# Loading w1 first as four full rows a partition, and three smaller edits, in a fused decode attention and Mish MLP kernel

## The chip, the cores and the metric

The kernel runs on one core of a Trainium2 chip. The metric is the time of one execution on the device in microseconds. Times of operations, waits and transfers are from the hardware profile of one execution of the kernel before the change.

## The reference

For 8 sequences with one new token each, the block adds to its input an attention over a long cache and a two-layer MLP, both fed with the same layer norm. All tensors are float32. Cut to what matters:

```python
x                # [8, 1, 512]
k_cache, v_cache # [8, 8, 8192, 128]   268 MB each
wq, wo           # [512, 4096], [4096, 512]
w1, b1, w2       # [512, 1792], [1792], [1792, 512]

xn = layernorm(x)
q = (xn @ wq) in 32 heads of 128; four heads share one key/value head
p = softmax(q @ k_cache^T * 128**-0.5)
a = (p @ v_cache) @ wo
h = xn @ w1 + b1
m = (h * tanh(softplus(h))) @ w2
out = x + a + m
```

## The kernel before, in words

The host lays the arrays out, and the kernel streams them through on-chip memory once. One *unit* is one sequence and two of its eight key/value heads: 8.4 MB of keys and 8.4 MB of values, each brought in by one DMA over all 128 partitions, 64 KB a partition. There are 32 units.

On-chip, one tile `kv` holds 2.5 such loads a partition. Values go to its start (`V_AT`). Keys go alternately to two places (`K_AT`) that overlap by half: the upper half of the first is the lower half of the second. A key load therefore starts once half of the unit before it has been multiplied. A second tile, `ws`, holds one quarter of wq (2.1 MB).

The order of work is written by hand. A loop of 17 steps runs `odd(t)` and then `even(t)`, a unit each; its last step runs `last()` instead of `even`. In a unit, `scores` multiplies the two halves of the keys with the unit's weights `wk` (32 products, which appear as 64 instructions, since each float32 product is two); `softmax` works on the VectorE and ScalarE; `values` does the value products of the unit before; `turn` and the VectorE behind it bring the probabilities into the form that `values` needs. Loads are issued from the SP queue, in the program's order, and an issue waits until what it overwrites has been read. Because SP works through its list in order, a load that waits holds up the loads behind it.

The MLP is spread out around this:

- Ahead of the loop (the *prologue*) the layer norm of x is made and transposed to `xn4`, which holds x's rows p*4+i in partition p. `project` makes the first queries from the first quarter of wq. `x_rows` and `x_turn` make `x8`, a second transposed copy of x with zeros in it, in the form that w1's layout needs. Its constant is `hmask`.
- w1 comes in one DMA, queued behind the first unit's keys: every partition gets eight half rows (`W1R = 8`), into the place of the values, which is still free.
- `up` makes h from w1 in 32 products of 448 columns, in `even(0)`, between the first unit's softmax and its `turn`. The first load of values, which overwrites w1, is issued once `up` is done. h stays in the accumulator bank `H` until `mish` reads it in `odd(1)`.
- In `last()`, the four parts of wo and then w2 are loaded in six parts (14 rows a partition: 4, 4, 3, 2 and the last row in two halves), all of w2 into the upper half of the second key place. `down_long` multiplies the first four rows in products of 512 columns into `H`; then ScalarE copies `H` to `a_sb`, four products with `bsel` bring it to the accumulator `O`, and `down` adds rows 5 to 14 to `O` in products of 128 columns. VectorE adds x, and the result is stored.

```python
    for p, t in zip(parts[1:], w2_t[1:]):
        down(p[0], p[1], t, p[2], p[3])
    res = os
    nc.vector.tensor_add(res, O[:, :P], xres)
    nc.sync.dma_start(out, res)
```

Of the kernel before, what the change touches and what calls it, by code (L numbers as in the profile page):

```python
# [8 lines left out]
F32 = mybir.dt.float32  # L9
AF = mybir.ActivationFunctionType  # L10
ALU = mybir.AluOpType
AX = mybir.AxisListType

P = 128
B = 8
D = 512
# [8 lines left out]
G = 4  # L25
# [3 lines left out]
CC = D // P  # L29
FG = F // G  # L30
FT = 4
FP = FG // FT
Q = P // G
# [15 lines left out]
NJ = PL * HALF  # L49


W1R = 8
W2R = 7


# [3 lines left out]
W1_AT = 0  # L59
W2_AT = 2 * ROW  # L60
# [15 lines left out]
def kernel(  # L76
# [12 lines left out]
    nc = tc.nc  # L89
    PSUM = bass.MemoryType.PSUM  # L90

    const = ctx.enter_context(tc.tile_pool(name="const", bufs=1))
# [4 lines left out]
    kv = const.tile([P, PLACES], F32, name="kv")  # L97
    ws = const.tile([P, CC * BW], F32, name="ws")
# [4 lines left out]
    M = psum.tile([P, 512], F32, name="m")  # L103
    H = psum.tile([P, 512], F32, name="h")
# [12 lines left out]
    apart = const.tile([P, P], F32, name="apart")  # L117
    gsel = const.tile([G, G, B], F32, name="gsel")
    xn4 = const.tile([P, CC, B], F32, name="xn4")
    hmask = const.tile([P, 2], F32, name="hmask")  # L120
    qr = const.tile([P, DI, H2 * B], F32, name="qr")
    xres = const.tile([P, P], F32, name="xres")
    oT = const.tile([P, H2, B], F32, name="oT")
    oX = const.tile([P, NP, CC, 2, B], F32, name="oX")

    x8 = oX.rearrange("p m i h b -> p (m i h b)")[:, : W1R * 2 * B]
    x8 = x8.rearrange("p (i h b) -> p i h b", i=W1R, h=2)
    aT = const.tile([P, 2 * W2R, B], F32, name="aT")
    pt8 = const.tile([P, HALF, PL * TL, H2], F32, name="pt8")
    tr = const.tile([P, PL * TL, 32], F32, name="tr")  # L130

    wk = const.tile([P, DI, 2, NH * G, REP], F32, name="wk")
    xe = wk.rearrange("p i d k h -> p (i d k h)")[:B].rearrange("b (i s) -> b i s", i=W1R)

    def load_q(m):

        rows = wq.rearrange("j p f -> (j p f)").rearrange("(m p f) -> m p f", m=NP, p=P)
# [14 lines left out]
    for lo in range(0, FG, FG // 2):  # L152
        hi = lo + FG // 2
        nc.scalar.dma_start(b1_sb[:, lo:hi], b1.rearrange("(g f) -> g f", g=G)[:, lo:hi])
    nc.sync.dma_start(
        kv[:, K_AT[0] : K_AT[0] + ROW],
        kT[:NB].rearrange("j p f -> (j p f)").rearrange("(p f) -> p f", p=P),
    )
    w1_t = kv[:, W1_AT : W1_AT + 7168].rearrange("p (i f) -> p i f", i=W1R)


    make_identity(nc, ident)
# [7 lines left out]

    def more_constants():
        nc.vector.reduce_sum(mask, ident.rearrange("p (x d) -> p x d", x=NB), axis=AX.X)
        nc.vector.reduce_sum(
            hmask, ident.rearrange("p (c h q) -> p h c q", c=CC, h=2), axis=AX.XY
        )
        nc.vector.memset(O, 0.0)
        for g in range(4):

            src = ident.rearrange("p (c d u g h) -> p d u g c h", c=2, d=2, u=2, g=4)
            dst = perm[:, g].rearrange("p (d u g c h) -> p d u g c h", d=2, u=2, g=4, c=2)  # L180
            for d in range(2):
                nc.vector.tensor_copy(dst[:, d, :, g], src[:, d, :, g])
        nc.vector.reduce_sum(hsel, ident.rearrange("p (c h) -> p h c", h=H2), axis=AX.X)
        nc.vector.reduce_sum(
            isel, ident.rearrange("p (c t h) -> p t c h", t=TL, h=H2), axis=AX.XY
        )
        for d in range(2):
            nc.vector.reduce_sum(
                rsel[:, d * REP : (d + 1) * REP],
                ident.rearrange("p (c d k h) -> p d h c k", c=2, d=2, h=REP)[:, d],  # L190
                axis=AX.XY,
            )
        away = work.tile([P, H2], F32, name="away", bufs=1)
        nc.vector.tensor_scalar(away, rsel, -FAR, FAR, op0=ALU.mult, op1=ALU.add)
        for c in range(2):
            nc.vector.tensor_copy(
                apart.rearrange("p (c d k h) -> p c d k h", c=2, d=2, h=REP)[:, c],
                away.rearrange("p (d o h) -> p d o h", d=2, o=1).to_broadcast([P, 2, NH * G, REP]),
            )
        nc.vector.tensor_copy(  # L200
            gsel, ident[:G, :G].rearrange("p (g o) -> p g o", o=1).to_broadcast([G, G, B])
        )
# [31 lines left out]
            gmask.rearrange("p (o g) -> p o g", o=1).to_broadcast([P, NB, DG]),  # L234
        )

    def x_rows():

        for c in range(CC):
            nc.vector.tensor_copy(
                xe.rearrange("b i (c h q) -> b c i h q", c=CC, h=2)[:, c],
                xc[:, c * P : (c + 1) * P]
                .rearrange("b (o q i) -> b i o q", o=1, i=W1R)
                .to_broadcast([B, W1R, 2, P // CC // 2]),
            )

    def x_turn():
        for i in range(W1R):  # L250
            nc.tensor.transpose(M[:, 32 + i * B : 32 + (i + 1) * B], xe[:, i], ident[:B, :B])
        for g in range(G):
            nc.tensor.matmul(
                M[Q * g : Q * g + B, 256:384],
                ident[:B, :B],
                x_sb[:, g * P : (g + 1) * P],
                start=True,
                stop=True,
            )
        for h in range(2):  # L260
            nc.vector.tensor_scalar(
                x8[:, :, h],
                M[:, 32 : 32 + W1R * B].rearrange("p (i b) -> p i b", i=W1R),
                hmask[:, h : h + 1],
                None,
                op0=ALU.mult,
            )
        nc.vector.tensor_copy(xres, M[:, 256:384])

    selections_long()  # L270
    x_rows()
    more_constants()


# [194 lines left out]
    def up(w1_t, b1_sb):  # L469
        for g in range(G):  # L470
            nc.tensor.matmul(
                hp[Q * g : Q * g + B, :], gsel[:, g, :], b1_sb, start=True, stop=False
            )
        for i in range(W1R):
            for g in range(G):
                nc.tensor.matmul(
                    hp[Q * g : Q * g + B, :],
                    x8[:, i, g // 2],
                    w1_t[:, i, g % 2 * FG : (g % 2 + 1) * FG],
                    start=False,  # L480
                    stop=(i == W1R - 1),
                )
# [42 lines left out]
                stop=False,  # L525
            )

    def down_long(w):

        for j in range(G):  # L530
            nc.tensor.matmul(
                H[Q * j : Q * j + B, :],
                aT[:, j, :],
                w[:, j * D : (j + 1) * D],
                start=False,
                stop=True,
            )

    def down(lo, hi, w, g0, g1):
        n = (g1 - g0) * P  # L540
        for j in range(lo, hi):
            for g in range(g0, g1):
                at = (j - lo) * n + (g - g0) * P
                nc.tensor.matmul(
                    O[Q * g : Q * g + B, :P],
                    aT[:, j, :],
                    w[:, at : at + P],
                    start=False,
                    stop=(j == 2 * W2R - 1),
                )  # L550

# [10 lines left out]
    def load(name, at, m, b):  # L562
        nc.sync.dma_start(place(at), units[name][m, b])  # L563

    nc.sync.dma_start(w1_t, w1.rearrange("j p f -> (j p f)").rearrange("(p i f) -> p i f", p=P, i=W1R))
    nc.sync.dma_start(place(K_AT[1])[:, ROW // 2 :], units["k"][0, 1][:, ROW // 2 :])
    project(work.tile([P, 512], F32, name="e", bufs=1))
    load_q(1)
    x_turn()
    spread()  # L570
    key_weights(0, 2)

    def last():

        w_o = [kv[:, 4096 * m : 4096 * (m + 1)] for m in range(NP)]
        for m in range(NP):
            rows = wo[4 * m : 4 * (m + 1)].rearrange("u p f -> (u p f)")
            rows = rows.rearrange("(p f) -> p f", p=P)
            nc.sync.dma_start(w_o[m], rows)
        w2_rows = w2.rearrange("j p f -> (j p) f").rearrange("(q i) f -> q (i f)", i=W2R)  # L580
        w2_t = []
        parts = ((0, G, 0, G), (G, 8, 0, G), (8, 11, 0, G), (11, 13, 0, G), (13, 14, 0, 2), (13, 14, 2, G))
        for lo, hi, g0, g1 in parts:
            a, z = (lo * D, hi * D) if g1 - g0 == G else (lo * D + g0 * P, lo * D + g1 * P)
            t = kv[:, W2_AT + a : W2_AT + z]
            nc.sync.dma_start(t, w2_rows[:, a:z])  # L586
            w2_t.append(t)

        values(place(K_AT[0]))
        for m in range(NP):  # L590
            if m == 1:
                merge(1, B - 1)
                turn_o(NP - 1)
            outputs(m, w_o[m])
        down_long(w2_t[0])
        a_sb = work.tile([P, 512], F32, name="e", bufs=1)
        nc.scalar.copy(a_sb, H)
        for g in range(G):
            nc.tensor.matmul(
                O[Q * g : Q * g + B, :P],  # L600
                bsel[:, :B],
                a_sb[:, g * P : (g + 1) * P],
                start=True,
                stop=False,
            )
        for p, t in zip(parts[1:], w2_t[1:]):
            down(p[0], p[1], t, p[2], p[3])
        res = os
        nc.vector.tensor_add(res, O[:, :P], xres)  # L609
        nc.sync.dma_start(out, res)  # L610
# [24 lines left out]
    def even(t):  # L635
# [14 lines left out]
        with tc.If(t > 0):  # L650
            values(place(V_AT))
        key_weights((2 * t + 1) % B)
        with tc.If(t == 0):  # L653
            up(w1_t, b1_sb)
        load("v", V_AT, t // 4 % NP, 2 * t % B)
        with tc.If(t % 4 - t // B * 4 == 3):
            load_q((t // 4 + 2) % NP)
# [49 lines left out]
```

## Time and profile before

| | |
|---|---|
| three runs: median (lowest to highest) | 1310.69 us (1310.49 to 1312.02) |
| the profiled execution | 1309.59 us |
| its span in the profile | 1307.8 us |
| TensorE busy, matmul | 992.6 us, 76% |
| VectorE busy | 359.0 us, 27% |
| DMA bytes | 561.33 MB, mean 429 GB/s |

Busy times are sums over the span, and the engines work side by side. A time at the start of a row of the timeline is microseconds from the start of the span. "xN" counts instructions, and a bracket at the end of a row gives how long the engine had been idle and what ended that. A row of SPq is the issue of a load; "to landing" is the time from the issue to the last byte.

### The profile page before, as it was taken

The numbers are of one execution on the slowest core, as the hardware profiler recorded it, in microseconds if no ns is written. First come the engines' busy times: TensorE is split into PE (matmuls) and PEld (weight loads), VectorE is DVE, ScalarE is ACT, GpSimd is POOL, SyncE is SP. The second block draws the span as 40 slices with busy tenths as digits, with TensorE's granted clock in tenths as the row PEclk, the third lists the DMA queues.
The fourth block names the chain that finished last, engine by engine and source line by source line (L and its number), as shares of the span: only waits on it lengthen the run. The fifth ranks groups of instructions, "written<-read, shape, count | busy, mean of one in ns | idle before, by whom it ended". The sixth has DMA issues, their size and how long they took to land. (4 is left out here: it accounts for less than half of the span.)

```text
span 1307.8 us, 15745 instructions
## 1 busy us (share of the span) xinstructions
PE 992.6 (76%) x4948; PEld 359.8 (28%) x4948; DVE 359.0 (27%) x654; ACT 39.3 (3%) x89; POOL 2.3 (0%) x10
## 2 busy tenths in 40 slices
PE   4887788778678688786686878878686878868686
PEld 2232223222222223222232322223232232323222
DVE  3215233221223302233312323212233231323312
ACT  1000000000000000000000000000000000000000
POOL 0000000000000000000000000000000000000000
PEclk9988898898888988998998888889888898988888
DMA  9999999999999999999999999999999999999998
GB/s 404 436 414 426 438 425 443 423 441 427 439 429 437 429 437 433 429 439 429 437 429 439 429 437 425 441 427 439 427 439 427 439 429 437 431 435 433 433 422 336
DMA packets 11857, 561.33 MB, mean 429 GB/s; under 512 B 1328, under 2 KB 1720, under 8 KB 1984
## 3 DMA queue, kind: packets, MB, share of 16 engines
q1 hardware_dynamic: 11680, 560.03, 99.2%
q10 hardware_dynamic: 160, 1.06, 0.2%
q8 instruction: 13, 0.21, 0.1%
q14 instruction: 4, 0.03, 0.0%
HBM read 561.01 MB, written 0.07 MB: 429 GB/s over the span
## 5 line engine op out<-in xcount | busy, mean ns | idle before, releaser
L373 PE MATMUL s<-kv,wk 128*64 128x512 f32 x2048 | 538.0, 664 | 195.7 <-DMA kv<-in_kT 108.2
L373 PEld LDWEIGHTS s<-kv,wk 128*64 128x64 f32 x2048 | 180.5, 151 | 521.7 <-issue 459.8
L428 PE MATMUL o<-kv,pt 128*32 128x512 f32 x2048 | 257.6, 659 | 31.1 <-DMA kv<-in_v 26.2
L385 DVE TENSOR_REDUCE nm<-s 128x1 f32<-128x512 f32 x32 | 22.1, 692 | 529.0 <-PE s L373 350.7
L399 PE MATMUL x<-e,perm 128*128 128x512 f32 x256 | 117.6, 602 | 26.5 <-PEq L653 15.0
L428 PEld LDWEIGHTS o<-kv,pt 128*32 128x32 f32 x2048 | 80.5, 120 | 184.8 <-issue 178.6
L408 DVE STREAM_TRANSPOSE tr<-x 128x512 f32<-128x512 f32 x128 | 79.2, 676 | 26.0 <-PE x L399 18.6
L435 DVE TENSOR_SCALAR os<-o,isel 128x128 f32<-128x128 f32 x32 | 11.2, 351 | 230.9 <-PE o L428 205.8
L399 PEld LDWEIGHTS x<-e,perm 128*128 128x128 f32 x256 | 46.0, 190 | 97.2 <-issue 96.9
L356 DVE TENSOR_TENSOR wk<-qr,mask 128x1024 f32<-128x1024 f32 (+1 forms) x34 | 65.1, 1915 | 12.9 <-DVEq L625 6.8
L393 ACT ACTIVATE e<-s,nmx 128x512 f32<-128x512 f32 x32 | 22.0, 687 | 1016.6 <-DVE nmx L390 1016.6
L417 DVE TENSOR_TENSOR pt<-tr 64x512 f32<-64x512 f32 x64 | 43.9, 687 | 4.4
L386 PE MATMUL m<-ident,nm 128*128 128x128 f32 x64 | 18.4, 375 | 28.4 <-DVE nm L385 28.4
L413 DVE TENSOR_TENSOR tr<-tr 128x1024 f32<-128x1024 f32 x32 | 39.2, 1225 | 1.1
L437 DVE SCALAR_TENSOR_TENSOR os<-o,isel,os 128x128 f32<-128x128 f32 x96 | 33.7, 351 | 3.4
L386 PEld LDWEIGHTS m<-ident,nm 128*128 128x128 f32 x64 | 11.4, 222 | 62.3 <-DVE nm L385 62.3
L442 PE MATMUL m<-hsel,os 128*128 128x8 f32 x64 | 10.9, 242 | 9.8 <-DVE rt L406 9.7
L442 PEld LDWEIGHTS m<-hsel,os 128*128 128x128 f32 x64 | 10.8, 189 | 19.4 <-DVE rt L406 11.3
L394 DVE TENSOR_SCALAR lsel<-rsel,l 128x8 f32<-128x8 f32 x32 | 7.4, 231 | 29.7 <-ACT e L393 15.8
L388 DVE TENSOR_TENSOR far<-m,apart 128x128 f32<-128x128 f32 x32 | 9.3, 292 | 21.3 <-PE m L386 21.3
L326 DVE TENSOR_SCALAR qT<-m 128x64 f32<-128x64 f32 x3 | 0.7, 225 | 51.1 <-PE m L319 51.1
L337 PE MATMUL x<-tr,gwide 128*128 128x512 f32 x16 | 10.9, 768 | 4.3 <-ACT qr L344 2.9
(106 smaller groups left out, 153.1 us busy)
## 6 DMA issues: line engine op xcount, KB each, us to landing
kv<-in_kT SPq DMA_DIRECT2D x2, 4096.0 KB, 32.8
kv<-in_wo SPq DMA_DIRECT2D x4, 2048.0 KB, 19.7
ws<-in_wq SPq DMA_DIRECT2D x3, 2048.0 KB, 33.3
kv<-in_w SPq DMA_DIRECT2D x1, 3584.0 KB, 35.5
kv<-in_w SPq DMA_DIRECT2D x2, 1024.0 KB, 27.6
ws<-in_wq ACTq DMA_DIRECT2D x1, 1024.0 KB, 5.1
ws<-in_wq SPq DMA_DIRECT2D x1, 1024.0 KB, 7.2
kv<-in_w SPq DMA_DIRECT2D x1, 768.0 KB, 26.4
```

The source lines that it names most:

```text
L356: nc.vector.tensor_mul(w[:, i : i + n], q[:, i : i + n].to_broadcast([P, n, 2, NH * G, REP]), mask.rearrange("p (o d k r) -> p o d k r", o ...
L373: nc.tensor.matmul(S[64 * c : 64 * (c + 1), :], w[:, i].rearrange("p d k h -> p (d k h)"), kk[:, i, c, :], start=(part == 0 and n == 0), s ...
L385: nc.vector.tensor_reduce(nm, S, axis=AX.X, op=ALU.max, negate=True)
L386: nc.tensor.matmul(M[:, 0:P], nm.to_broadcast([P, P]), ident, start=True, stop=True)
L393: nc.scalar.activation(e, S, AF.Exp, bias=nmx, accum_out=l)
L399: nc.tensor.matmul(X[:, g], perm[:, g], e, start=True, stop=True)
L408: nc.vector.transpose(tr.rearrange("p (l t) c -> p t l c", t=TL)[:, tl], X.rearrange("p g (t q l) -> p t l g q", t=TL, q=PP)[:, tl],)
L413: nc.vector.tensor_add(t[:, :, 0], t[:, :, 0], t[:, :, 1])
L417: nc.vector.tensor_add(pt8[half, :, :, d * REP : (d + 1) * REP].rearrange("p c y h -> p y c h"), t[:, 0], t[:, 1],)
L428: nc.tensor.matmul(O[Q * q : Q * (q + 1), :], pt8[:, c, TL * l : TL * (l + 1), :].rearrange("p t h -> p (t h)"), vt[:, 512 * n : 512 * (n ...
L437: nc.vector.scalar_tensor_tensor(os, O[:, DH * i : DH * (i + 1)], isel[:, i : i + 1], os, op0=ALU.mult, op1=ALU.add)
L442: nc.tensor.matmul(M[:, 168 : 168 + H2], os, hsel, start=True, stop=True)
```

## The change: w1 first, and its products in the prologue

Four edits:

1. w1's load is issued ahead of the first keys instead of behind them, and in another form. A partition now gets four full rows (`W1R = 4`), which are the rows that `xn4` already pairs with it. Since w1 lies in memory by blocks of 128 rows and by halves of its columns, it is now four DMAs, each into 32 of the 128 partitions, two runs of 14,336 bytes a partition. Before it was one DMA into 128 partitions, 28,672 bytes each.
2. `up` moves from `even(0)` to the prologue, and has 16 products instead of 32. `x8`, `xe`, `hmask`, `x_rows` and the eight transposes of `x_turn` are gone.
3. In `last()`, rows 5 to 8 of w2 are multiplied by `down_long` (4 products of 512 columns) instead of `down` (16 of 128). The copy of `H` comes behind them, and `down` does rows 9 to 11 ahead of the `bsel` products instead of behind.
4. w2's last row goes to `ws` instead of `kv`.

```diff
-W1R = 8
+W1R = CC
...
+    w1_t = kv[:, W1_AT : W1_AT + 7168].rearrange("p (h i f) -> p h i f", h=2, i=W1R)
+    for c in range(CC):
+        nc.sync.dma_start(
+            w1_t[Q * c : Q * (c + 1)].rearrange("q h i f -> q h (i f)"),
+            w1[2 * c : 2 * (c + 1)].rearrange("h (q i) f -> q h (i f)", i=W1R),
+        )
     nc.sync.dma_start(
         kv[:, K_AT[0] : K_AT[0] + ROW],
         kT[:NB].rearrange("j p f -> (j p f)").rearrange("(p f) -> p f", p=P),
     )
-    w1_t = kv[:, W1_AT : W1_AT + 7168].rearrange("p (i f) -> p i f", i=W1R)
...
                 nc.tensor.matmul(
                     hp[Q * g : Q * g + B, :],
-                    x8[:, i, g // 2],
-                    w1_t[:, i, g % 2 * FG : (g % 2 + 1) * FG],
+                    xn4[:, i, :],
+                    w1_t[:, g // 2, i, g % 2 * FG : (g % 2 + 1) * FG],
...
-    nc.sync.dma_start(w1_t, w1.rearrange("j p f -> (j p f)").rearrange("(p i f) -> p i f", p=P, i=W1R))
     nc.sync.dma_start(place(K_AT[1])[:, ROW // 2 :], units["k"][0, 1][:, ROW // 2 :])
     project(work.tile([P, 512], F32, name="e", bufs=1))
     load_q(1)
     x_turn()
+    up(w1_t, b1_sb)
     spread()
...
-            t = kv[:, W2_AT + a : W2_AT + z]
+            t = kv[:, W2_AT + a : W2_AT + z] if lo < 13 else ws[:, a - 13 * D : z - 13 * D]
...
-        down_long(w2_t[0])
+        down_long(0, G, w2_t[0])
+        down_long(G, 2 * G, w2_t[1])
         a_sb = work.tile([P, 512], F32, name="e", bufs=1)
         nc.scalar.copy(a_sb, H)
+        down(*parts[2][:2], w2_t[2], 0, G)
...
-        for p, t in zip(parts[1:], w2_t[1:]):
+        for p, t in zip(parts[3:], w2_t[3:]):
             down(p[0], p[1], t, p[2], p[3])
...
-        with tc.If(t == 0):
-            up(w1_t, b1_sb)
```

The order shows the first place on the SP queue, at the start of the program. `in_x`, `in_wq`, `in_kT` and `in_w` are x, wq, the keys and w1. `DMAHWn_49` is one of eight counters that the loads take in turn, and `PE_49` the count of TensorE's work. Before:

```order
L145 DMA tr<-in_x 8x512
L149 DMA ws<-in_wq 128x2048
L155 DMA kv<-in_kT 128x16384
L565 DMA kv<-in_w 128x7168
L566 DMA kv<-in_kT 128x8192
L138 DMA ws<-in_wq 128x4096 [waits DMAHW2_49,DMAHW0_49,PE_49]
```

And now:

```order
L140 DMA tr<-in_x 8x512
L144 DMA ws<-in_wq 128x2048
L152 DMA kv<-in_w 32x2x3584 x3
L152 DMA kv<-in_w 32x2x3584 [waits DMAHW0_49]
L156 DMA kv<-in_kT 128x16384 [waits DMAHW1_49]
L540 DMA kv<-in_kT 128x8192 [waits DMAHW2_49]
L133 DMA ws<-in_wq 128x4096 [waits DMAHW3_49,PE_49]
```

w1 has moved ahead of both key loads and become four loads. With three more loads in the list, the counters come round earlier: the fourth part of w1 waits for the half of wq that ScalarE issued, the first keys for x, and the other keys for SP's half of wq.

The second place is TensorE in the prologue. `h` is the accumulator `H`, `m` a small scratch accumulator, `x_69` the bank that `spread` uses. Before:

```order
L280 MATMUL h<-ws,xn_86 8x512 x4
L290 MATMUL m<-bsel,e 128x8 x4
L251 MATMUL m<-ident,wk 128x8 x8
L253 MATMUL m<-tr,ident 8x128 x4
L337 MATMUL x_69<-tr,gwide 128x512 x2
```

And now:

```order
L254 MATMUL h<-ws,xn_86 8x512 x4
L264 MATMUL m<-bsel,e 128x8 x4
L236 MATMUL m<-tr,ident 8x128 x4
L445 MATMUL h<-kv,gsel 8x448 x4
L450 MATMUL h<-kv,xn_86 8x448 x16
L311 MATMUL x_69<-tr,gwide 128x512 x2
```

The eight transposes are gone, and the 20 products of `up`, of which the first 4 add b1 and the other 16 wait for w1, stand ahead of `spread`.

The third place is TensorE in `last()`, behind the products with wo. `aT` is the activated h, `kv` holds w2. Before:

```order
L531 MATMUL h<-kv,aT 8x512 x4
L599 REGISTER_ALU
L599 MATMUL o<-e,bsel 8x128 x4
L544 REGISTER_ALU
L544 MATMUL o<-kv,aT 8x128 x16
L544 REGISTER_ALU
L544 MATMUL o<-kv,aT 8x128 x12
L544 REGISTER_ALU
L544 MATMUL o<-kv,aT 8x128 x8
L544 REGISTER_ALU
L544 MATMUL o<-kv,aT 8x128 x2
```

And now:

```order
L506 MATMUL h<-kv,aT 8x512 x4
L506 REGISTER_ALU
L506 MATMUL h<-kv,aT 8x512 x4
L519 REGISTER_ALU
L519 MATMUL o<-kv,aT 8x128 x12
L576 REGISTER_ALU
L576 MATMUL o<-e,bsel 8x128 x4
L519 REGISTER_ALU
L519 MATMUL o<-kv,aT 8x128 x8
L519 REGISTER_ALU
L519 MATMUL o<-ws,aT 8x128 x2
```

Sixteen short products have become four long ones, and the `bsel` products stand one part of w2 later.

More of the change, by code (lines that the diff above doesn't have):

```diff
@@ L119 @@
     xn4 = const.tile([P, CC, B], F32, name="xn4")
-    hmask = const.tile([P, 2], F32, name="hmask")
     qr = const.tile([P, DI, H2 * B], F32, name="qr")
@@ L124 @@
     oX = const.tile([P, NP, CC, 2, B], F32, name="oX")
-    x8 = oX.rearrange("p m i h b -> p (m i h b)")[:, : W1R * 2 * B]
-    x8 = x8.rearrange("p (i h b) -> p i h b", i=W1R, h=2)
     aT = const.tile([P, 2 * W2R, B], F32, name="aT")
@@ L132 @@
     wk = const.tile([P, DI, 2, NH * G, REP], F32, name="wk")
-    xe = wk.rearrange("p i d k h -> p (i d k h)")[:B].rearrange("b (i s) -> b i s", i=W1R)
     def load_q(m):
@@ L172, in more_constants @@
         nc.vector.reduce_sum(mask, ident.rearrange("p (x d) -> p x d", x=NB), axis=AX.X)
-        nc.vector.reduce_sum(
-            hmask, ident.rearrange("p (c h q) -> p h c q", c=CC, h=2), axis=AX.XY
-        )
         nc.vector.memset(O, 0.0)
@@ L235, in selections_long @@
         )
[L237 to L247, printed above, removed]
     def x_turn():
-        for i in range(W1R):
-            nc.tensor.transpose(M[:, 32 + i * B : 32 + (i + 1) * B], xe[:, i], ident[:B, :B])
         for g in range(G):
@@ L259, in x_turn @@
             )
[L260 to L267, printed above, removed]
         nc.vector.tensor_copy(xres, M[:, 256:384])
     selections_long()
-    x_rows()
     more_constants()
@@ L526, in outputs, with down_long @@
             )
-    def down_long(w):
-        for j in range(G):
+    def down_long(lo, hi, w):
+        for j in range(lo, hi):
+            g = j % G
             nc.tensor.matmul(
-                H[Q * j : Q * j + B, :],
+                H[Q * g : Q * g + B, :],
                 aT[:, j, :],
-                w[:, j * D : (j + 1) * D],
+                w[:, (j - lo) * D : (j - lo + 1) * D],
                 start=False,
-                stop=True,
+                stop=(j >= 2 * G - G),
             )
@@ L547, in down @@
                     w[:, at : at + P],
-                    start=False,
+                    start=(j == 2 * G),
                     stop=(j == 2 * W2R - 1),
@@ L602, in last @@
                 a_sb[:, g * P : (g + 1) * P],
-                start=True,
+                start=False,
                 stop=False,
             )
-        for p, t in zip(parts[1:], w2_t[1:]):
+        for p, t in zip(parts[3:], w2_t[3:]):
             down(p[0], p[1], t, p[2], p[3])
```

## Prediction

> **What bounds the kernel now.** I read the page first, then stretches of the span, then the end of the chain of waits.
>
> ```profile
> span 1307.8 us, 15745 instructions
> PE 992.6 (76%) x4948; PEld 359.8 (28%) x4948; DVE 359.0 (27%) x654; ACT 39.3 (3%) x89; POOL 2.3 (0%) x10
> GB/s 404 436 414 426 438 425 443 423 441 427 439 429 437 429 437 433 429 439 429 437 429 439 429 437 425 441 427 439 427 439 427 439 429 437 431 435 433 433 422 336
> q1 hardware_dynamic: 11680, 560.03, 99.2%
> ```
>
> No engine is full: TensorE, the busiest, works 76% of the span. The transfers are: SP's queue keeps the 16 DMA engines busy for 99.2% of it, and the rate is level but for the first and the last slice.
>
> ```profile
> 60.00:100.00 40.00, 29.21 (x152) 10.74 (x150) 11.75 (x23) 0.78 (x2) 0.00 (x0) 0.87 0.99 416
> 100.00:1200.00 1100.00, 843.21 (x4092) 304.12 (x4094) 306.45 (x532) 29.37 (x69) 0.00 (x0) 0.89 1.00 433
> ```
>
> A row gives the stretch, each engine's busy time, the granted clock, the DMA share and the rate. From 100 to 1200 us the DMA share is 1.00 at 433 GB/s: the next load is always queued before the last has ended. The chain of waits agrees; its last long pieces are landings.
>
> ```profile
> 1204.84 31.16 DMA kv<-in_kT
> 1245.56 29.14 DMA kv<-in_v
> 1275.10 18.09 DMA kv<-in_w
> ```
>
> So the end is the start of the stream, plus all bytes at the rate of the stream, plus holes, plus what follows the last landing. Work saved on an engine counts only if it closes a hole. Between 60 and 100 us the rate is 416: (433 - 416) x 40 / 433 = 1.6 us lost, the only stretch here with something to win.
>
> **The change: order of the loads.** These are SP's issues, and the landings of the first keys, of w1 (3584 KB), and of wq's second quarter (the longest of three).
>
> ```profile
> 1.62 0.42 SPq L155 DMA_DIRECT2D kv<-in_kT  x1
> 2.08 0.64 SPq L565 DMA_DIRECT2D kv<-in_w  x1
> 2.77 0.60 SPq L566 DMA_DIRECT2D kv<-in_kT  x1
> 14.85 0.33 SPq L138 DMA_DIRECT2D ws<-in_wq  x1
> 40.74 0.34 SPq L643 DMA_DIRECT2D kv<-in_kT  x1
> 57.31 0.35 SPq L563 DMA_DIRECT2D kv<-in_v  x1
> 78.14 0.35 SPq L563 DMA_DIRECT2D kv<-in_kT  x1
> ```
>
> ```profile
> L155 SPq DMA_DIRECT2D kv<-in_kT x1: 419/419/419, 1.6 to 1.6; - x1
> DMA to landing us min/median/max: 26.6/26.6/26.6
> ...
> kv<-in_w SPq DMA_DIRECT2D x1, 3584.0 KB, 35.5
> ...
> L138 SPq DMA_DIRECT2D ws<-in_wq x3: 328/333/333, 14.9 to 602.8; - x3
> DMA to landing us min/median/max: 33.0/33.3/37.3
> ```
>
> The first keys land at 1.62 + 26.6 = 28.2 us, w1 at 2.08 + 35.5 = 37.6. Its 3.67 MB take 3.67 / 0.433 = 8.5 us of the stream. Swapping two loads in one queue moves no byte: at the same rate the swap costs the stream 0, and the first keys land at 28.2 + 8.5 = 36.7 us. Three more issues of about 0.6 us each (L565's row) on SP, and waits for x and wq, delay no data: the queue then holds 2.1 MB of wq and three parts of w1.
>
> **The change: form of w1's load.** This is the large unknown. Every large load of the trace writes all 128 partitions; now four loads write 32 each, one behind the other. No row shows how fast such a load is. The near bound is w1's own row: the same bytes on the same queue, 8.5 us, so no loss, if the 433 GB/s belong to the 16 engines alone. A gain is excluded, since the engines run at their steady rate already. The far bound is a rate that goes with the partitions written: 433 x 32 / 128 = 108 GB/s, 34 us, a loss of 25.4. The row nearest in kind is the near bound, but what it shares with the new loads is everything except what changes. A rate this level over keys, values and weights looks like a fixed ceiling, which can lie in the engines or on the way into the partitions. With neighbouring partitions sharing a way in, a quarter of them would reach some of the ways and not all. Between factors 1 and 4 I take 2: 17 us, a loss of 8.5.
>
> The Trainium skill speaks against the change here (SBUF — State Buffer, "Door 1: The DMA port swizzle"): partitions are reached through 16 ports, partitions 0 to 31 and 32 to 63 through the same eight, the others through the other eight, and two transfers do not combine, so it gives about 218 GB/s. By that, an estimate from its figure, w1 takes 16.8 us; by the row of w1's one load, 8.5. No run here shows which holds.
>
> **The change: prologue and the first unit.** One fence holds TensorE, ScalarE and VectorE rows.
>
> ```profile
> 8.12 1.27 DVE L242 COPY wk<-tr 8x256 f32<-8x256 f32 x4
> 18.70 0.61 PE L253 MATMUL m<-tr,ident 8*8 8x128 f32 x8
> 20.70 2.07 PE L337 MATMUL x<-tr,gwide 128*128 128x512 f32 x2 [1.39 <-DVE tr L332]
> 26.18 1.06 DVE L356 TENSOR_TENSOR wk<-qr,mask 128x512 f32<-128x512 f32 x1 [1.69 <-ACT qr L344]
> 31.37 9.25 PE L373 MATMUL s<-kv,wk 128*64 128x512 f32 x32 [5.85 <-PEq L663]
> 49.87 0.93 PE L471 MATMUL h<-kv,gsel 4*8 4x448 f32 x8 [0.64 <-PEq L650]
> 49.99 0.69 ACT L393 ACTIVATE e<-s,nmx 128x512 f32<-128x512 f32 x1 [23.85 <-DVE nmx L390]
> 50.73 6.20 PE L476 MATMUL h<-kv,oX 128*8 128x448 f32 x64
> 56.86 3.70 PE L399 MATMUL x<-e,perm 128*128 128x512 f32 x8
> ```
>
> The copies of `x_rows` (1.27 us) and the transposes go; the work behind them already waited for nothing they hold up, since the first scores started 3.2 us after the keys' landing. `up` shrinks from 64 + 8 instructions to 32 + 8: 0.93 + 6.20 / 2 = 4.0 us. It waits for w1, which follows wq in the queue: before, the first keys did, and their 8.39 / 0.433 = 19.4 us began at 28.2 - 19.4 = 8.8. At 17 us w1 ends near 25.8. `up`, with b1's products done by then, ends near 29, the two `spread` products start there instead of at 20.70, and `wk` is ready 8.3 us later than 26.18 + 1.06 = 27.2, at 35.5. The first keys land at 45.2 in that case (36.7 with a full rate, where `wk` is later by some 1.5 us only). The cover is the keys' landing, with 8 to 10 us to spare; without it `up` would cost its 4.0.
>
> The first unit then runs from that landing. Before, 56.86 - 31.37 = 25.5 us lay between the first scores and `turn`; without `up` the latter needs only e, ready at 49.99 + 0.69, so 19.3 us. At full rate `turn` starts at 36.8 + 19.3 = 56.1 instead of 56.86: what the swap takes, taking `up` out returns.
>
> Two loads hang on this chain. The lower half of the second keys is issued once the first 9.25 us of scores are done: at 46.2 (full rate) against 40.74 before, while wq's quarter ahead of it lands at 14.85 + 37.3 = 52.2. A margin of 11.5 us becomes 6; it stays the same with slow loads, since both move. The first values no longer wait for `up`, and follow at once. The third keys (78.14) come 0.7 us earlier relative to the stream. Their lateness shows:
>
> ```profile
> 80.00:82.00 2.00, 2.00 (x12) 0.86 (x10) 0.00 (x0) 0.00 (x0) 0.00 (x0) 1.00 0.67 229
> ```
>
> Of two microseconds 0.67 are used, so 0.7 us are lost; I book a gain of 0.3, bounds 0 and 0.7.
>
> **The change: the end.**
>
> ```profile
> 1297.57 1.14 PE L531 MATMUL h<-kv,aT 128*8 128x512 f32 x8
> 1299.03 0.58 ACT L597 COPY e<-h 128x512 f32<-128x512 f32 x1 [36.77 <-PE h L531]
> 1299.66 0.41 PE L599 MATMUL o<-e,bsel 128*8 128x128 f32 x8 [0.96 <-ACT e L597]
> 1299.89 1.06 PE L544 MATMUL o<-kv,aT 128*8 128x128 f32 x32
> 1301.20 0.84 PE L544 MATMUL o<-kv,aT 128*8 128x128 f32 x24 [0.26 <-DMA kv<-in_w]
> 1302.47 1.02 PE L544 MATMUL o<-kv,aT 128*8 128x128 f32 x24 [0.42 <-DMA kv<-in_w]
> ```
>
> TensorE waits for w2's parts at 1301.20 and at 1302.47. Rows 5 to 8 cost 1.14 us in long products (L531) against 1.06 in short ones. The copy of `H` moves behind them, to about 1300.7 to 1301.3, under the wait and rows 9 to 11; the `bsel` products (0.41) follow at 1302.05 and end at 1302.46, just as rows 12 and 13 land. Cost 0, bounds -0.1 and +0.4 (the 0.41 exposed). The last row's place in `ws` changes no byte and no wait that is late: 0.
>
> **Sum.** Against the profiled execution: 1309.59 + 0 (swap) + 8.5 (form) - 0.3 (third keys) + 0 (end) = 1317.8. The median of the runs stands 1.1 us above it: 1318.9 us. About 0.2% (2.6 us) is what a measurement of this kernel can tell from no change.
>
> **Rivals.** *Full rate for 32 partitions.* Then the form costs 0, and 1310.69 - 0.3 = 1310.4: no change, the other side of the line. For it: the 99.2% share names the DMA engines as busy, and a load spread over all 16 would keep them so. It decides from a rate above 3.67 / (8.5 + 2.6) = 331 GB/s in w1's load. *A rate by partitions.* 108 GB/s, 25.4 us lost, 1335.8; nothing in the rows speaks for so sharp a fall. *Loads that overlap in part.* The engines drift apart, some on the third part while others are on the first, and half the loss comes back: 4.2 us, 1314.6. *A late second half of the keys.* If the first scores started more than 6 us behind the landing (before: 3.2 with code that had to be reached first), a hole opens, 1 to 2 us for each as many beyond: 1312 at full rate. *Faster.* All holes between 60 and 100 us closed at full rate give 1.6 us, 1309.1, which is still no change; beyond the line I know no mechanism.
>
> **How the numbers follow.** Half rate 0.62, overlap in part 0.06, partition rate 0.03: slower 0.71, with 0.01 for a hole. Full rate 0.24, same. An unseen gain 0.04. The range runs from 1309.5 to 1320.8: below, the full-rate case, which at 0.24 can't be left out; above, half rate with the end's 0.4, a lost third-keys gain and 1.2 us of spread between runs. The half-rate case alone has 1316 to 1320.8.
>
> **What would show it.** Half rate: w1's four loads move some 217 GB/s from 9 to 26 us, the page's first rate falls from 404 to near 290, and the first scores start near 45. Full rate: the first scores near 36.8 and a first slice as before. In both, `up` in 4.0 us, the first values issued right behind the second keys, an unchanged end. I am wrong if w1's load runs above 331 GB/s, or if the stream has new holes after 60 us.

## The result, and the profile after

| | before | after |
|---|---|---|
| median (lowest to highest) | 1310.59 us (1310.30 to 1313.12) | 1319.99 us (1317.00 to 1323.29) |
| the profiled execution | 1309.59 us | 1323.29 us |

The ratio is 1.0069, 95% interval 1.0050 to 1.0087: slower by 0.7%. The forecast was 1318.9. The profiled execution of the changed kernel is the slowest of the six, so its profile holds more than the change; a later profile of the same kernel at 1315.90 us is read beside it below. A spread of this size is not the change's own: 26 later runs of the kernel before lie from 1307.93 to 1314.85 us.

The page of the changed kernel: span, engines, rate in 40 slices, and two queues (packets, MB, share).

```profile
span 1321.5 us, 15482 instructions
PE 960.6 (73%) x4884; PEld 347.2 (26%) x4884; DVE 357.2 (27%) x647; ACT 39.3 (3%) x89; POOL 2.3 (0%) x10
GB/s 279 427 440 423 437 436 428 436 431 433 434 429 438 431 425 441 435 425 437 434 427 437 439 423 436 427 415 443 439 419 439 442 420 436 441 423 434 441 415 307
q1 hardware_dynamic: 11856, 560.03, 99.0%
q8 instruction: 38, 0.62, 0.2%
```

TensorE has 32 us less work and the kernel is slower: the transfers still set the time. The first slice fell from 404 to 279 GB/s. The last row counts packets of code. The page of the kernel before has

```profile
q8 instruction: 13, 0.21, 0.1%
```

so 25 packets of 16 KB came in addition. Three stretches of the changed kernel (the last two columns are DMA share and GB/s):

```profile
10.00:24.00 14.00, 9.28 (x48) 4.11 (x40) 2.83 (x12) 1.17 (x2) 0.00 (x0) 1.00 1.01 210
60.00:100.00 40.00, 28.55 (x134) 10.18 (x134) 10.07 (x16) 1.55 (x4) 0.00 (x0) 0.91 1.02 435
100.00:1200.00 1100.00, 817.17 (x4120) 296.12 (x4109) 304.69 (x533) 29.39 (x69) 0.00 (x0) 0.88 1.00 433
```

While w1 comes, the engines are as busy as ever (1.01) and move 210 GB/s, against 433 later. w1's 3.67 MB then take 3.67 / 0.210 = 17.5 us instead of 8.5. A busy share near 1 does not say that bytes flow at full rate: the packets themselves took longer. In the trace, w1's 256 packets of 14,336 bytes took 1.12 us each (median), and the fastest of them 0.54 us.

SP's issues and TensorE in the prologue and the first unit:

```profile
1.62 4.56 SPq L152 DMA_DIRECT2D kv<-in_w  x4
6.23 0.43 SPq L156 DMA_DIRECT2D kv<-in_kT  x1
9.59 0.35 SPq L540 DMA_DIRECT2D kv<-in_kT  x1
56.63 0.34 SPq L620 DMA_DIRECT2D kv<-in_kT  x1
65.64 0.36 SPq L538 DMA_DIRECT2D kv<-in_v  x1
```

```profile
27.40 5.00 PE L450 MATMUL h<-kv,xn 128*8 128x448 f32 x32 [6.34 <-DMA kv<-in_w]
32.33 1.13 PE L311 MATMUL x<-tr,gwide 128*128 128x512 f32 x2
47.36 9.16 PE L347 MATMUL s<-kv,wk 128*64 128x512 f32 x32 [12.10 <-DMA kv<-in_kT]
66.81 3.67 PE L373 MATMUL x<-e,perm 128*128 128x512 f32 x8 [1.69 <-ACT e L367]
```

`up` (L450) waits for w1 and runs at 27.40; the first scores wait for the keys until 47.36, with TensorE idle for 12.10 us: the keys' landing still covers what moved ahead of it. The first values (65.64) do not follow the second keys (56.63) at once: SP waits another 6.9 us for TensorE to reach the branch ahead of the value products (L627), which stands behind the unit's scores. The queue was not empty in that time: from 56 to 66 us the rate was 447 GB/s. The end:

```profile
1311.34 1.04 PE L506 MATMUL h<-kv,aT 128*8 128x512 f32 x8
1313.05 1.04 PE L506 MATMUL h<-kv,aT 128*8 128x512 f32 x8 [0.67 <-DMA kv<-in_w]
1314.40 0.58 ACT L573 COPY e<-h 128x512 f32<-128x512 f32 x1 [45.60 <-PE h L506]
1314.92 0.84 PE L519 MATMUL o<-kv,aT 128*8 128x128 f32 x24 [0.82 <-DMA kv<-in_w]
1315.58 0.40 PE L576 MATMUL o<-e,bsel 128*8 128x128 f32 x8
1316.18 0.62 PE L519 MATMUL o<-kv,aT 128*8 128x128 f32 x16 [0.19 <-DMA kv<-in_w]
```

TensorE waits for w2's parts ahead of three groups, where before it was two; the copy and the `bsel` products (L576) fit between.

### The profile page after: what moved, and what is told of

Same layout as the page of the kernel before. It is cut to its first block, busy times and chain, and to the rows that moved or that the text cites. A ratio compares the mean times of both kernels' runs of the same rounds, so it can differ in the third digit from the quotient of the medians.

```text
span 1321.5 us, 15482 instructions
## 1 busy us (share of the span) xinstructions
PE 960.6 (73%) x4884; PEld 347.2 (26%) x4884; DVE 357.2 (27%) x647; ACT 39.3 (3%) x89; POOL 2.3 (0%) x10
## 3 DMA queue, kind: packets, MB, share of 16 engines
q10 hardware_dynamic: 160, 1.06, 0.2%
## 5 line engine op out<-in xcount | busy, mean ns | idle before, releaser
L347 PE MATMUL s<-kv,wk 128*64 128x512 f32 x2048 | 524.3, 670 | 244.2 <-DMA kv<-in_kT 179.6
L402 PE MATMUL o<-kv,pt 128*32 128x512 f32 x2048 | 243.3, 630 | 34.4 <-DMA kv<-in_v 34.4
L402 PEld LDWEIGHTS o<-kv,pt 128*32 128x32 f32 x2048 | 75.6, 115 | 178.6 <-issue 176.9
L416 PEld LDWEIGHTS m<-hsel,os 128*128 128x128 f32 x64 | 10.8, 189 | 19.2 <-DVE rt L380 11.0
L362 DVE TENSOR_TENSOR far<-m,apart 128x128 f32<-128x128 f32 x32 | 9.3, 292 | 19.1 <-PE m L360 19.1
L494 PE MATMUL h<-kv,oX 128*8 128x512 f32 x64 | 9.1, 689 | 3.1 <-DMA kv<-in_wo 3.1
```

Of the source, the lines that this page charges most:

```text
L347: nc.tensor.matmul(S[64 * c : 64 * (c + 1), :], w[:, i].rearrange("p d k h -> p (d k h)"), kk[:, i, c, :], start=(part == 0 and n == 0), s ...
L402: nc.tensor.matmul(O[Q * q : Q * (q + 1), :], pt8[:, c, TL * l : TL * (l + 1), :].rearrange("p t h -> p (t h)"), vt[:, 512 * n : 512 * (n ...
L416: nc.tensor.matmul(M[:, 168 : 168 + H2], os, hsel, start=True, stop=True)
```

## The experiments

### Where the 8.5 us come from: the form of w1's load

The first theory: neighbouring partitions share a way in, so 32 of them run at half rate. `form32` is the kernel before with this edit alone, in the old place of the queue:

```diff
-    nc.sync.dma_start(w1_t, w1.rearrange(...))
+    for c in range(4):
+        nc.sync.dma_start(w1_t[Q * c : Q * (c + 1)], w1_rows[Q * c : Q * (c + 1)])
```

> The kernel before, with w1's one load of 128 partitions made four loads of 32 neighbouring partitions, at its old place behind the first keys; nothing else. Theory A (a load into 32 partitions runs at half the stream's rate, about 208 GB/s, and the stream has no slack): 8.4 us more, 1319.0 us, w1's packets twice as long, the first scores where they were before, 31.4. Theory B (the loss of the changed kernel comes from the later start of the first unit): no loss here, 1310.6 us. Both: 13 packets on the queue that brings code, as before.

Measured: 1318.68 us, ratio 1.0060 (1.0044 to 1.0076) to 1310.48. The form alone costs 8.2 us; neither full rate, nor a rate by partitions, nor an overlap that gives half back. The first scores did not stay at 31.4 us: they began at 34.71, behind a longer wait at the branch ahead of them (9.13 us against 5.85). w1's stretch in this profile:

```profile
28.00:44.00 16.00, 9.29 (x32) 3.11 (x32) 0.00 (x0) 0.00 (x0) 0.00 (x0) 1.00 1.01 210
```

`form64` is the same with two loads of 64 neighbours:

```diff
+    for c in range(2):
+        nc.sync.dma_start(w1_t[64 * c : 64 * (c + 1)], w1_rows[64 * c : 64 * (c + 1)])
```

> The kernel before with one edit: w1's one load becomes two loads of 64 neighbouring partitions each, in the old place of the queue, same bytes. Theory A (neighbouring partitions share a way in, and 0 to 63 use the same half of the ways as 0 to 31): both halves still run at some 210 to 220 GB/s, so the loss is the same as with four parts, 8.2 us: about 1318.7. Theory B (the rate goes with the number of partitions written, and 32 happened to give a half): 64 partitions run at the full 433 GB/s, no loss: 1310.5. Theory C (a cost of each separate load): half as many parts, half of the loss, 1314.6, with the stream at full rate between the parts.

Measured: 1319.38 us, ratio 1.0063 (1.0048 to 1.0079) to 1310.65, +8.7. Twice the partitions, no faster. In the profile of `form64`, w1's stretch:

```profile
28.00:44.00 16.00, 9.51 (x32) 3.04 (x32) 0.00 (x0) 0.00 (x0) 0.00 (x0) 1.00 1.00 208
```

`form32_spread` has four loads of 32 partitions again, but every fourth one:

```diff
+    for c in range(4):
+        nc.sync.dma_start(w1_t[c::4], w1_rows[c::4])
```

> The kernel before with one edit: w1's one load becomes four loads of 32 partitions each, but every fourth partition (0, 4, 8 and so on) and not 32 neighbours. Its first part waits for the first keys to land, so the time has a delay of its own and is not the reading; the rate while w1 comes is. Theory A (neighbours share a way in): the 32 partitions of a load now reach all ways, and w1's stretch runs at some 430 GB/s. Theory B (the number of partitions counts): 210 to 220 GB/s as with 32 neighbours.

One execution: 1310.80 us. Its loads were issued from 27.78 to 30.30 us, with the first keys landed, and stand next in the queue, which had run nearly empty by then (12 GB/s from 26 to 28 us); its packets run from 29.1 to 39.7 us. Two stretches from the middle of that:

```profile
32.00:34.00 2.00, 0.84 (x2) 0.32 (x4) 0.00 (x0) 0.00 (x0) 0.00 (x0) 1.00 1.04 438
34.00:36.00 2.00, 2.00 (x8) 0.78 (x6) 0.00 (x0) 0.00 (x0) 0.00 (x0) 1.00 1.00 430
```

The same bytes, the same number of loads and of partitions a load, and the full rate. The DMA records of the traces show it packet by packet; w1 comes in 128 packets of 28,672 bytes in all four kernels:

| run | partitions of one load | a packet, median | first packet's start to last one's end |
|---|---|---|---|
| before | all 128 | 1.06 us | 10.5 us |
| `form32` | 32 neighbours | 2.23 us | 19.1 us |
| `form64` | 64 neighbours | 2.23 us | 19.9 us |
| `form32_spread` | 32, every fourth | 1.06 us | 10.6 us |

So neither the number of partitions nor the number of loads makes the half rate, but that the partitions of a load are neighbours within one half (32 or 64 of them; neighbours across the middle were not run). The edits also change the order in which w1 is read from memory. That this makes the half rate is unlikely, though no run separates it: `form64` reads 1.8 MB in one piece a load, and a quarter of wq, 2.1 MB in one piece, goes into 128 partitions at full rate (16,384 bytes in 0.61 us). By the rule of the Trainium skill (SBUF — State Buffer, "Door 1: The DMA port swizzle"), 0 to 31 and 32 to 63 go through the same eight of 16 ports. These three runs agree with it; its 218 GB/s stand against 208 and 210 here.

### The order of the loads, and the products in the prologue

`swap` is the kernel before with w1's one load issued ahead of the first keys; `up` stays in the first unit.

```diff
+    nc.sync.dma_start(w1_t, w1.rearrange(...))
     nc.sync.dma_start(kv[:, K_AT[0] : K_AT[0] + ROW], ...)
...
-    nc.sync.dma_start(w1_t, w1.rearrange(...))
```

> The kernel before, with w1's load in its old form (one load, 128 partitions, eight half rows) issued ahead of the first keys; its products stay in the loop. Theory A: no byte moves and the stream stays full, 1310.6 us within 1.5; the first keys land near 36.7. As the first unit starts 5.5 us later and still holds the products with w1, holes after 80 us may cost 1 to 4 us. Theory B: the later start costs all it delays, 1316 to 1319 us.

Measured: 1314.79 us, ratio 1.0031 (1.0018 to 1.0044), +4.3. A row each of its TensorE, its SP queue and its rate:

```profile
56.75 6.20 PE L477 MATMUL h<-kv,oX 128*8 128x448 f32 x64
```

```profile
63.33 0.35 SPq L564 DMA_DIRECT2D kv<-in_v  x1
```

```profile
60.00:64.00 4.00, 4.00 (x35) 1.39 (x28) 0.00 (x0) 0.00 (x0) 0.00 (x0) 1.00 0.04 14
```

The first unit runs later, `up` (L477) ends at 62.95, and only then may the first values overwrite w1. For 4 us the queue is all but empty (14 GB/s), a loss of (433 - 14) x 4 / 433 = 3.9 us and so most of the 4.3.

`rows128` is the changed kernel with w1 laid out by the host so that the four full rows of each partition come in one load over all 128; all else as in the change.

```diff
+    nc.sync.dma_start(w1_t, w1.rearrange(...))
...
-        "w1": lay(inputs["B_w1"], (CC, P, 2, F // 2), (0, 2, 1, 3), (2 * CC, P, F // 2)),
+        "w1": lay(inputs["B_w1"], (D, F), (0, 1), (2 * CC, P, F // 2)),
```

> The changed kernel, with the host laying w1 out so that its four full rows a partition come in one load of 128 partitions; all else as changed. Theory A: the half rate is gone. What is left over the kernel before is the code that TensorE fetches again in each step of the loop (38 packets of 16 KB on the code queue instead of 13, each about 1 us on one of 16 DMA engines): if the extra 25 fall on few engines, 1311.5 to 1315 us; if they spread evenly, 25/16 = 1.6 us and 1311.9. Rival: 0.4 MB more of 561 cost nothing, 1310.3 us.

Measured: 1307.82 us (1306.25 to 1313.87), ratio 0.9990 (0.9975 to 1.0006); both expectations lay above that. The second keys, the first values and the third keys in it:

```profile
47.49 0.34 SPq L616 DMA_DIRECT2D kv<-in_kT  x1
56.41 0.35 SPq L534 DMA_DIRECT2D kv<-in_v  x1
79.33 0.35 SPq L534 DMA_DIRECT2D kv<-in_kT  x1
```

With `up` in the prologue the values go out at 56.41 instead of 63.33 (57.31 before), and the hole of `swap` is gone. The swap costs nothing because the products moved with it; the change without its form of load is level with the kernel before, or a little below.

### The end

`tail` is the kernel before with the two edits of `last()` alone.

> The kernel before with the two edits at the end alone: rows 5 to 8 of w2 in 512-column products ahead of the copy of H, and w2's last row in wq's buffer; w1's load, its place and its products as before. The prediction booked 0 for both, bounds -0.1 and +0.4: 1310.5 to 1310.9. Rival: the copy and the bsel products, now behind rows 5 to 8, come out late, and the products of rows 12 and 13 wait for them: +0.4 to +1. A second rival: part of the 2.7 us by which the full-rate version of the change stood below the kernel before comes from here: 1308 to 1309.5.

Measured: 1309.81 us, ratio 0.9992 (0.9982 to 1.0001). The cost is nothing, and no gain is shown either.

### Code that is fetched again

The branch of line L640 parts `even` from `last()`: a step meets it ahead of `even` and again behind it, where it jumps over `last()` to the loop's end. It shows what the 25 extra packets did. TensorE's row of this branch, changed kernel (count, then min/median/max in ns):

```profile
L640 PEldq COMPARE_BRANCH  x33: 67/332/8047, 43.1 to 1283.4; - x33
```

Sixteen of the 33 took over 6 us (114 us together), one in all but one of the 17 steps, with some two packets of code a step. In the kernel before it is two:

```profile
L665 PEldq COMPARE_BRANCH  x33: 68/169/7332, 30.7 to 1275.1; - x33
```

Theory D: the place of the shorter program's loop in memory makes these fetches. `rows128_dead` is `rows128`, and `after_dead` the changed kernel, with products that are never carried out, so that TensorE's loop ends where it did before:

```diff
+        with tc.If(t % 4 + t // 4 * 4 == 19):
+            for n in range(36):
+                nc.tensor.matmul(hp[...], xn4[:, n // G % CC, :], w1_t[...], start=False, stop=False)
```

> As the kernel with one load of w1's full rows, with 36 products in the loop under a condition that is never true, so that TensorE's code behind them lies as far from its start as in the kernel before. Nothing more is executed than one branch a step. Theory A (repeated fetches come from where the loop's code lies): 13 or so code packets and 1310.3 us. Rival (they come from something else that the change does): 38 packets as without the padding, and the same time as without it.

Measured: 1308.47 us, ratio 0.9982 (0.9973 to 0.9992), 6 packets. But `rows128` itself, whose TensorE program is nearly that of the changed kernel, had only 5: there was nothing to cure.

> The changed kernel with 36 products added to the body of the loop that are never carried out (their condition never holds), so that TensorE's loop ends where it ended in the kernel before (instruction 1548 against 1546, and 1394 in the changed kernel). Theory D (the place of the loop's code makes the repeated fetches, and these cost the 4 us that the changed kernel has over its parts): 13 packets or fewer, no long stall of the branch after the first steps, 1316. Theory E (nothing to do with the place): the same count and time as the changed kernel of this job.

Measured: 1317.99 us (1317.49 to 1320.75), ratio 1.0060 (1.0046 to 1.0073), 6 packets. Beside it the changed kernel itself, as `again`:

> The changed kernel once more, without an edit. Its first profile showed 25 more code packets than the kernel before (38 against 13), two in nearly every step of the loop. Theory D (the program fetches code again in each step because of where its loop lies): some 38 packets again, median near 1320 and runs as far apart as before (1317 to 1323). Theory E (one execution happened to start so): some 5 to 13 packets, no long stall of the loop's branch, and a median of 1310.5 + 8.2 (form) - 2.7 (the full-rate version's gain) = 1316.

Measured: 1320.22 us (1318.33 to 1323.34), ratio 1.0080 (1.0066 to 1.0094); its profiled execution, the fastest of the five, had 10 packets. The intervals of `again` and `after_dead` overlap. Both theories missed: the same program has 38 packets in one execution and 10 in another, so the place alone does not decide; and the median did not fall to 1316 as E wanted. Three more profiles were taken, two of the changed kernel and one of `rows128`.

> The changed kernel, one execution with its profile. Two profiled executions so far: 38 code packets at 1323.29 us, 10 at 1318.33. If the repeated fetches make the runs' spread, time goes with the count here: 1318 to 1319 near 10 packets, 1322 to 1323.5 near 38, in between for a count in between. If not, the time stands apart from the count.

> The same once more: another pair of count and time. By the theory that the fetches make the spread, each packet costs (1323.29 - 1318.33) / 28 = 0.18 us over ten of them.

> The full-rate version of the change once more with its profile. Eight of its twelve runs lay at 1306.3 to 1308.1 and four at 1312.3 to 1313.9; the profiled one was of the first kind, with 5 code packets. If repeated fetches make the second kind, this one shows either 5 to 10 packets near 1307.5 or some 35 near 1313.

Measured: 1315.90 with 5 packets, 1318.37 with 5, and 1310.06 with 5. Time does not simply go with the count. To see what else differs, each execution is cut at two issues of SP and one landing: the second load of values, and the last one with its landing (from the chain). In the profiled execution of the changed kernel and in `after_p1`:

```profile
103.58 0.34 SPq L538 DMA_DIRECT2D kv<-in_v  x1
...
1258.62 29.82 DMA kv<-in_v
```

```profile
102.71 0.34 SPq L538 DMA_DIRECT2D kv<-in_v  x1
...
1252.62 28.49 DMA kv<-in_v
```

So the loop between the issues took 1258.62 - 103.58 = 1155.04 us there and 1149.91 here; all executions cut alike:

| execution | code packets | second values issued | to the last values' issue | to landing | rest | time |
|---|---|---|---|---|---|---|
| before | 13 | 94.09 | 1151.47 | 29.14 | 34.89 | 1309.59 |
| changed, first profile | 38 | 103.58 | 1155.04 | 29.82 | 34.85 | 1323.29 |
| `again` | 10 | 102.41 | 1151.40 | 29.76 | 34.76 | 1318.33 |
| `after_p1` | 5 | 102.71 | 1149.91 | 28.49 | 34.79 | 1315.90 |
| `after_p2` | 5 | 106.56 | 1147.94 | 28.77 | 35.10 | 1318.37 |
| `rows128` | 5 | 95.35 | 1147.93 | 29.89 | 34.79 | 1307.96 |
| `rows128_p` | 5 | 98.59 | 1147.71 | 28.92 | 34.84 | 1310.06 |

An issue may stand a microsecond or two earlier or later against the stream, so the border of the first two parts is soft; their sum is not. In the changed kernel that sum is 1252.62 and 1254.50 us with 5 packets, 1253.81 with 10 and 1258.62 with 38. Two things vary. The loop takes 1147.7 to 1149.9 us where no code comes again after the first steps, some 1151.4 with 10 or 13 packets, and 1155.0 with 38. And the start varies by 4 us between two executions of one program. The second scores of `after_p1` and `after_p2`, and the row of the branch in the latter:

```profile
77.73 8.70 PE L347 MATMUL s<-kv,wk 128*64 128x512 f32 x32 [8.11 <-DVEq L597]
```

```profile
80.43 9.86 PE L347 MATMUL s<-kv,wk 128*64 128x512 f32 x32 [9.43 <-issue]
```

```profile
L640 PEldq COMPARE_BRANCH  x33: 67/169/8100, 43.2 to 1276.5; - x33
```

In `after_p2` the first long branch of L640 took 8.10 us (6.78 in `after_p1`), the scores began 2.7 us later, the keys that wait for them went out later too, and from 92 to 94 us the stream stood almost still:

```profile
92.00:94.00 2.00, 2.00 (x12) 0.78 (x10) 0.00 (x0) 0.00 (x0) 0.00 (x0) 1.00 0.16 66
```

What makes one execution fetch its loop again in each step and the next one not is open. That the fetches cost the 5 us between 1155.0 and 1149.9 rests on one execution with 38 packets, and is not shown by an experiment that switches them on or off.

## Why the prediction was right

- *Bound.* Right. 32 us less of TensorE's work gave nothing, and the column "rest" (34.8 to 35.1 in seven executions) shows that the time is the landing of the last values plus a constant.
- *Form of w1's load, +8.5.* Right in mechanism, and in size where it stands alone: 8.2 (`form32`), 8.7 (`form64`). Inside the change it is less sharp: 7.9 between the fastest profiles of `rows128` and of the changed kernel (1315.90 - 1307.96), but 12.2 between their medians (1319.99 - 1307.82), and 9.5 between the padded ones (1317.99 - 1308.47). w1's packets stretch over 18.4 to 19.2 us in four executions of the changed kernel and over 9.1 us in `rows128`, 9 to 10 us more. The rest of the 12.2 is open. The term was a choice between 0 and 25.4, and no row gave the factor 2; what carried it was that a ceiling as level as 433 GB/s may lie on the way into the partitions. Forecast rate some 217 GB/s, measured 210; first slice near 290, measured 279; first scores near 45, measured 47.4, of which some 1.5 because w1 came later than forecast (`up` began at 27.40; its w1 was expected near 25.8).
- *Swap, 0.* Right, and for the stated reason: without the move of `up` it would have been +4.3.
- *First values right behind the second keys.* Wrong: 9.0 us behind them (65.64 against 56.63), and 8.9 in `rows128` (56.41 against 47.49). The step looked at `up` alone and missed that the issue also waits for TensorE to pass the first unit's scores. It cost nothing, because the queue still held work.
- *`up`, 4.0 us under the keys' landing.* The 4.0 were 0.93 for b1's products and 3.1 for w1's. The former took 1.72 us, ahead of w1's landing, and the latter 5.00: one instruction took 913 ns (median) against 539 before, at a granted clock of 1.00 in both, and why is open. As 12.1 us of idle time stood behind it, the cost was 0 as booked.
- *Third keys, -0.3.* Not borne out. The term rested on third keys that go out 0.7 us earlier against the stream; in `rows128`, where the stream ahead of them has the same bytes and rate, they went out at 79.33 us, and at 82.58 in `rows128_p`, against 78.14 before. The stretch from 60 to 100 us went from 416 to 435 GB/s in the changed kernel, but 416 stands in `rows128` too, which has the same order of loads:

```profile
60.00:100.00 40.00, 28.77 (x152) 10.50 (x150) 11.04 (x21) 0.78 (x2) 0.00 (x0) 0.87 0.98 416
```

  With the slow form alone (`form32`) it is 437, but 432 at full rate in `form32_spread`, and two executions of one program differ as much: 437 in `after_p1` and 418 in `after_p2`. So no gain of the change can be read from this stretch.
- *End, 0.* Right: `tail`, and the column "rest".
- *What it lacked.* "New holes after 60 us" were named as what would make it wrong, and in part they came: at 92 us in `after_p2`, and 3.6 us in the loop of the first profile against the kernel before. The range took 1.2 us for the spread of runs, and runs of the changed kernel lie from 1315.90 to 1323.34.
- *The sum.* That it came out within 1.1 us is in part luck. Without the form it gives 1310.4, and `rows128` measured 1307.82, 2.6 less; the form then made 12.2 of it instead of 8.5, 3.7 more. The two misses nearly cancel. The first is not clear of noise, as the interval of `rows128` holds "no change" and its runs fall into two groups, eight up to 1308.07 us and four from 1312.30 on. What parts the groups, and what makes the 3.7 us, no run here shows.

## What to carry to other kernels

Before a load is split by partitions, ask which partitions each part writes: here 32 or 64 neighbours cost half of the rate, and every fourth partition cost none, so that a split need not cost rate if the parts interleave. Look at the issues then, too: the interleaved loads waited 25.7 us for the first keys to land, which the neighbouring ones did not. A load may go ahead in a queue only if the reader that frees its buffer goes ahead too, or the next load waits for it (14 GB/s for 4 us in `swap`). And where runs of one kernel lie 7 us apart, take more than one profile before a difference is given to the change, and compare medians with medians as well as one profile with another.

## What the hardware showed unexpectedly

One and the same program fetched 38, 10, 5 and 5 packets of code in four executions. The Trainium skill (Runtime: NRT & Kernel Launch, "Instruction fetch mechanics") has code come in blocks of 16 KiB, and a branch out of the present window force a fetch. The size agrees (0.62 MB in 38 packets); that the branch at the loop's end fetches in every step was seen in one execution of four. Such a branch held TensorE for 6 to 8 us. Most of that cost no time: the sixteen of the first profile add up to 114 us, and that execution was 5 to 7.4 us longer than the other three.
